# Linear attention, then a mixture-of-depths MLP: the MLP pipeline a slot earlier, the first batch's rows by a 0/1 product, loads reordered

## The chip, the cores and the metric

One NeuronCore of a Trainium2 chip (its five engines: TensorE, VectorE, ScalarE, GpSimd, and SyncE, which here only issues DMAs). The metric is the device time of one execution in microseconds. In the profile PE is TensorE's matmuls, PEld its weight loads, DVE VectorE, ACT ScalarE, POOL GpSimd, SP SyncE.

## The reference

Eight batches, eight heads, 576 positions, head dimension 64, all float32; the MLP has 512 x 1024 and 1024 x 512 weights and runs on 128 chosen rows of each batch.

```python
q_s = softmax(q, axis=-1)                    # over the 64 features
k_s = softmax(k, axis=2)                     # over the 576 positions
kv = np.einsum('bhsd,bhse->bhde', k_s, v)    # 64 x 64 for each head
x = np.einsum('bhsd,bhde->bhse', q_s, kv)    # then heads side by side: (8, 576, 512)
...
scores = np.einsum('bsd,d->bs', x, w_gate)
out = x.copy()
for b in range(B):
    top_idx = np.argpartition(-scores[b], capacity)[:capacity]     # capacity = 128
    xe = x[b, top_idx]
    ye = np.maximum(xe @ w1, 0.0) @ w2
    g = 1.0 / (1.0 + np.exp(-scores[b, top_idx]))
    out[b, top_idx] = x[b, top_idx] + g[:, None] * ye
```

## The kernel before

The work is cut into 16 *units*: a batch and four of its eight heads, so units 2b and 2b+1 make batch b. `q`, `k` and `v` of a unit lie in one of three sets of buffers (`raw`, `LD = 3`), so unit u + 3 can be loaded once unit u is read. Each unit goes through these steps:

- `load`: six DMAs on SP's queue (two each for k, v and q, 256 and 320 KB); unit 0's v goes out on ScalarE's queue.
- `k_exp`, `q_exp` (ScalarE): exponentials, k in one instruction, q in two halves; `v_copy`: v into a buffer `v_ones` that has a column of ones beside it, on VectorE or GpSimd. There are two of these buffers.
- `kv_mm` (TensorE): k and v into a PSUM bank of the tag `tp`, of which there are two; the column of ones gives the sums of k. `kv_out`: VectorE's `krec` (1/sum), ScalarE's copy to `kv_w`, then VectorE's `prod` and a reduction with the gate weights `wg`, which give the score of each row as one more column. `kv_and_exp(u)` puts `kv_mm`, half of `q_exp`, `kv_out` and the other half in this order.
- `q_t` (TensorE transposes, in two halves, and a scaled copy of each on ScalarE), `x_mm` (TensorE, two halves), `x_out` (VectorE: reciprocal, scaled rows into `xs`, score part into `sr`), `x_store`: two DMAs of the rows to the output.

Once for each batch, after its second unit: `score` (VectorE sums, and two small operations that blank rows that aren't there; GpSimd splits the score in parts of bfloat16), `score_row` (five TensorE transposes with one score column each, into two `tp` banks, and two ScalarE copies to `srow`), `compare` (five VectorE instructions that count for each row how many scores stand before it: its rank), `pick` (VectorE's `hit`, a 0/1 matrix of rank against slot number in a single buffer; five small matmuls that give the row numbers and scores of the chosen rows; GpSimd's gather of the rows from the output tensor), `gate` (the sigmoid), `turn` (four transposes of the gathered rows, copied to `xT`).

The MLP on 128 rows goes in sixteen *pieces*: eight of `mlp1` (four matmuls each, half of `hT` written by ScalarE after every four) and eight of `mlp2` (one matmul each). `finish` (VectorE's `o`, then GpSimd's scatter) ends a batch.

The order on each engine is that of the program text (`manual_schedule`). Engines run their own instructions in order, and a wait holds up everything behind it on the same engine. Slots 0 to 3 (the loop at L520, `EARLY = 4`) hold only attention, one unit each, with dummy matmuls (`fill`) between, like the 20 at the start (`WARM`); slot 2 holds the first pick. From slot 4 on (the loop at L571, `LAG = 4`) each slot holds one unit's attention between eight pieces: `mlp1` of a batch in an even slot, `mlp2` in an odd one. In such a slot the next unit's exponentials and `kv_mm` are done too; `score` stands in the odd slot, `score_row` and `compare` in the even slot after, `pick` in the odd slot after that, two pieces in. Slots 16 to 19 have only the MLP left. In slot 16 the range checks `sums_in_range` (L470) are emitted after the eight `mlp1` pieces of batch 6: twelve small VectorE operations and one matmul that sums the flags. At the end a register takes a branch by them, to a general version that doesn't run here.

The MLP's weights are loaded in slots 0 to 3: `w1` in four row blocks, `w2` in two halves. The gate weights are spread over the partitions by two DMAs of 64 KB on ScalarE's queue.

Of the kernel before, what the change touches and what calls it, by code (L numbers as in the profile page):

```python
# [17 lines left out]
def kernel(  # L18
# [20 lines left out]
    nc = tc.nc  # L39
# [18 lines left out]
    WARM = 20  # L58
# [4 lines left out]
    n_sl = -(-capacity // P)  # L63
    cuts = [capacity * i // n_sl for i in range(n_sl + 1)]
# [27 lines left out]
    def load(u, which, queue=nc.sync):  # L92
        b, qd = units[u]
        for what in which:
            src = {"q": q, "k": k, "v": v}[what]
            t = raw[what][u % LD]
            first = src[b, 4 * qd].offset
            for n, rows in ((1, N2), (0, R)):
                queue.dma_start(
                    out=t[n::2, :, :rows].rearrange("p h r d -> p h (r d)"),  # L100
                    in_=bass.AP(tensor=src.tensor, offset=first + n * R * D,
                                ap=[[9 * D, 64], [SD, 4], [1, rows * D]]))
# [5 lines left out]
    load(0, "k")  # L108
    load(0, "v", nc.scalar)
    load(0, "q")  # L110
    load(1, "kvq")
    load(2, "kvq")

# [7 lines left out]

    wg = const.tile([P, NQ, 2, D], F32, name="wg")
    for h in range(2):
        nc.scalar.dma_start(out=wg[part(h)].rearrange("p a i d -> p (a i) d"),
                            in_=bass.AP(tensor=moe_w_gate.tensor, offset=moe_w_gate.offset + h * D,
                                        ap=[[0, 64], [2 * D, 2 * NQ], [1, D]]))
    warm = const.tile([P, 1], F32, name="warm")
    nc.scalar.activation(out=warm, in_=ones_b[:, :1], func=AF.Exp)
    w1 = const.tile([P, KD, F], F32, name="w1")
    w2 = const.tile([P, KF, DM], F32, name="w2")  # L130

# [99 lines left out]
    def q_t(u, i):  # L231
# [5 lines left out]
        for r in range(R):  # L237
            for a in range(2):
# [3 lines left out]
        nc.scalar.activation(out=st["qT", u][:, i].rearrange("p r a c -> p a r c"),  # L242
                             in_=t_ps[:, :, :R * 64].rearrange("p a (r c) -> p a r c", r=R),
                             func=AF.Copy, scale=krec[:, u, i:i + 1])
# [14 lines left out]
    def x_out(u, i):  # L259
        b, qd = units[u]  # L260
        if qd == 0 and i == 0:
            xs[b] = xp.tile([P, R, NQ, 2, 2, D], F32, tag="xs", name="xs")
            sr[b] = md.tile([P, NQ * 2, G], F32, tag="sr", name="sr")
        x = st.pop(("x", u, i))[:, :, :R * C].rearrange("p h (r c) -> p h r c", r=R)
        rec = qrec[:, u, i].rearrange("p (h r) -> p h r", h=2)
        nc.vector.reciprocal(out=rec, in_=x[:, :, :, D])  # L266
        nc.vector.tensor_mul(xs[b][:, :, qd, i].rearrange("p r h d -> p h r d"), x[:, :, :, :D],  # L267
                             rec.to_broadcast([P, 2, R, D]))
        nc.vector.tensor_mul(sr[b][:, 2 * qd + i].rearrange("p (h r) -> p h r", h=2), x[:, :, :, D + 1], rec)
# [10 lines left out]
    def score(b, up=2):  # L280

        raw_s = s_all[:, b]
        nc.vector.reduce_sum(out=raw_s, in_=sr.pop(b).rearrange("p a (h r) -> p r a h", h=2),
                             axis=AX.XY)
        s = md.tile([P, R], F32, tag="s", name="s")
        nc.vector.tensor_mul(s, raw_s, valid_r[:, up])
        nc.vector.tensor_add(s, s, valid_r[:, 1])
# [8 lines left out]
    def score_row(b):  # L296
        s = st["s", b]
        srow = md.tile([P, RP], F32, tag="srow", name="srow")
        for r0, r1 in ((0, N2), (N2, R)):
            t_ps = bank("tp", 2)  # L300
            for r in range(r0, r1):
                nc.tensor.transpose(out=t_ps[:, (r - r0) * P:(r - r0 + 1) * P],
                                    in_=s[:, r:r + 1].to_broadcast([P, P]), identity=ident)
            if r0 == 0:
                nc.scalar.copy(out=srow[:, :N2 * P], in_=t_ps)
            else:
                nc.scalar.copy(out=srow[:, N2 * P:], in_=t_ps[:, :P:2])  # L307
# [43 lines left out]

    def gate(b, n):
# [9 lines left out]
    def turn(b, n):  # L362
        m = slots[n][1]
        xr = st["pick", b, n][0]
        xT = sl.tile([P, KD, P], F32, tag="xT", name="xT")
        t_ps = bank("mm", 2)
        for d in range(KD):
            nc.tensor.transpose(out=t_ps[:, d * m:(d + 1) * m], in_=xr[:m, d * P:(d + 1) * P],  # L368
                                identity=ident[:m, :m])
        nc.scalar.copy(out=xT[:, :, :m], in_=t_ps[:, :KD * m].rearrange("p (d c) -> p d c", d=KD))  # L370
# [67 lines left out]
    def general():  # L438
        for b in range(B):
# [16 lines left out]
            score_row(b)  # L456
# [33 lines left out]
    LAG = 4  # L490

    def load_w1(n):
        nc.sync.dma_start(out=w1[:, n], in_=moe_w1[n * P:(n + 1) * P])

    def load_w2(n):
        half = KF // 2
        nc.sync.dma_start(out=w2[:, n * half:(n + 1) * half],
                          in_=moe_w2[n * half * P:(n + 1) * half * P].rearrange("(f p) d -> p f d", p=P))

    EARLY = 4  # L500

# [12 lines left out]
    k_exp(0)  # L514
    v_copy(0)
    kv_and_exp(0)
    load(3, "kvq")


    for s in range(EARLY):  # L520
        q_t(s, 0)
        q_t(s, 1)
        k_exp(s + 1)
        v_copy(s + 1, nc.gpsimd)
        fill(2)
        x_mm(s, 0)
        x_mm(s, 1)
        fill(2)
        if s == 2:
            kv_mm(s + 1)  # L530
            q_exp(s + 1, 0)
            fill(3)
            pick(0)
            x_out(s, 0)
            kv_out(s + 1)
            x_out(s, 1)
            x_store(s)
            q_exp(s + 1, 1)
        else:
            x_out(s, 0)  # L540
            x_out(s, 1)
            x_store(s)
            if s == 1:
                score(0)
            kv_mm(s + 1)
            q_exp(s + 1, 0)
            kv_out(s + 1)
            if s == 1:
                score_row(0)
                for r in range(R):  # L550
                    compare(0, r)
            q_exp(s + 1, 1)
            if s == 3:
                score(1)
        fill(2)
        if s == 0:
            load_w1(0)
            load_w1(1)
        elif s == 1:
            load_w1(2)  # L560
            load_w1(3)
            load(4, "kvq")
            load(5, "kvq")
        else:
            load_w2(s - 2)
            load(s + 4, "kvq")
    each(gate, 0)
    each(turn, 0)

    number = None  # L570
    for s in range(EARLY, NU + LAG):  # L571

        mlp_b, odd = divmod(s - LAG, 2)
        piece = mlp2 if odd else mlp1
# [10 lines left out]
        last = s == NU - 1  # L585
        ends = s // 2 if here and odd else None
        compared = s // 2 - 1 if here and not odd else None
        chosen = (s - 3) // 2 if here and odd else B - 1 if s == NU else None
# [3 lines left out]
        if after:  # L592
            v_copy(s + 1)
            k_exp(s + 1)
        pieces(2)
        if chosen is not None:
            pick(chosen)
        if here:
            x_mm(s, 0)
            x_mm(s, 1)  # L600
            x_out(s, 0)
            x_out(s, 1)
            x_store(s)
        if last:
            score(ends)
        if after:
            kv_and_exp(s + 1)
        if s + 4 < NU:
            load(s + 4, "kvq")
        pieces(1)  # L610
        if last:
            compared = ends
        if compared is not None:
            score_row(compared)
            for r in range(R):
                compare(compared, r)
        if chosen is not None:
            each(gate, chosen)
        if ends is not None and not last:
            score(ends)  # L620
        pieces(4)
        if odd and mlp_b + 1 < B:
            each(turn, mlp_b + 1)
        pieces(1)
        if odd:
# [31 lines left out]
```

## Time and profile before

| | |
|---|---|
| median of three runs | 219.21 us (218.94 to 222.68) |
| the profiled execution | 217.89 us, span 216.0 us |
| TensorE waiting, matmuls from 42.6 to 209 us | 1.6 us in all |
| first `mlp1` matmul | 42.64 us |
| first gather (`xr`) | issued at 33.97 us; the transposes after it start at 41.24 us |
| last `mlp2` matmul ends | 208.79 us |
| bytes moved | 46.81 MB, mean 217 GB/s |

The costliest groups, line, engine, operation, tiles (written<-read), shapes and count, then busy time, mean duration in ns, and the idle time before them with what ended it:

```profile
L382 PE MATMUL mm<-xT,w 128*128 128x128 f32 x512 | 62.1, 278 | 0.0
L392 PE MATMUL mm<-w,hT 128*128 128x512 f32 x128 | 59.9, 603 | 0.0
L315 DVE SCALAR_TENSOR_TENSOR junk<-srow,s,not_before 128x576 bf16<-128x576 f32 x40 | 32.8, 819 | 8.3 <-ACT srow L307 7.2
L215 PE MATMUL tp<-v_ones,ke 128*64 128x65 f32 x640 | 22.6, 224 | 2.3 <-issue 2.1
L253 PE MATMUL x<-kv_w,qT 64*64 64x66 f32 x1280 | 22.4, 221 | 0.0
```

Two thirds of TensorE's time is the MLP (the two first groups). A float32 matmul is several records, and matmuls overlap, so the mean of one record is longer than its share of the stream: what a step costs is read from start to start in the timeline. In the slices of the page each digit is the busy tenths of a fortieth of the span, 5.4 us.

### The profile page before, as it was taken

The numbers are of one execution on the slowest core, as the hardware profiler recorded it, in microseconds if no ns is written. First come the engines' busy times: TensorE is split into PE (matmuls) and PEld (weight loads), VectorE is DVE, ScalarE is ACT, GpSimd is POOL, SyncE is SP. The second block draws the span as 40 slices with busy tenths as digits, with TensorE's granted clock in tenths as the row PEclk, the third lists the DMA queues.
The fourth block names the chain that finished last, engine by engine and source line by source line (L and its number), as shares of the span: only waits on it lengthen the run. The fifth ranks groups of instructions, "written<-read, shape, count | busy, mean of one in ns | idle before, by whom it ended". The sixth has DMA issues, their size and how long they took to land. (4 is left out here: it accounts for less than half of the span.)

```text
span 216.0 us, 7090 instructions
## 1 busy us (share of the span) xinstructions
PE 197.5 (91%) x3040; PEld 147.2 (68%) x3040; DVE 116.2 (54%) x359; ACT 88.6 (41%) x146; POOL 34.4 (16%) x78
## 2 busy tenths in 40 slices
PE   5987595999999999999999999999999989999960
PEld 2464462799749975897679776996599548749620
DVE  6552595668726774477626872596358665501010
ACT  2386374763626471746265443536263311211100
POOL 6022402300112012200320023001120112101010
PEclk9999999999999999999999999999999999999996
DMA  5999999999999997958594949421313041101001
GB/s 179 299 356 358 375 398 369 362 392 377 377 384 381 375 344 249 314 157 283 171 320 154 313 133 303 161 82 49 113 52 109 7 156 52 49 3 52 5 5 52
DMA packets 39335, 46.81 MB, mean 217 GB/s; under 512 B 2944, under 2 KB 36736, under 8 KB 39296
## 3 DMA queue, kind: packets, MB, share of 16 engines
q1 hardware_dynamic: 36928, 41.36, 56.4%
q0 software_dynamic: 1280, 4.20, 5.7%
q10 hardware_dynamic: 1088, 0.72, 1.1%
q8 instruction: 26, 0.43, 0.8%
q14 instruction: 13, 0.11, 0.2%
HBM read 34.73 MB, written 11.53 MB: 214 GB/s over the span
## 5 line engine op out<-in xcount | busy, mean ns | idle before, releaser
L382 PE MATMUL mm<-xT,w 128*128 128x128 f32 x512 | 62.1, 278 | 0.0
L382 PEld LDWEIGHTS mm<-xT,w 128*128 128x128 f32 x512 | 58.8, 192 | 2.3 <-ACT xT L370 1.5
L392 PE MATMUL mm<-w,hT 128*128 128x512 f32 x128 | 59.9, 603 | 0.0
L315 DVE SCALAR_TENSOR_TENSOR junk<-srow,s,not_before 128x576 bf16<-128x576 f32 x40 | 32.8, 819 | 8.3 <-ACT srow L307 7.2
L392 PEld LDWEIGHTS mm<-w,hT 128*128 128x128 f32 x128 | 22.5, 190 | 21.2 <-issue 20.4
L267 DVE TENSOR_TENSOR xs<-x,qrec 128x640 f32<-128x640 f32 x32 | 26.4, 825 | 1.1
L242 ACT ACTIVATE qT<-x,krec 128x640 f32<-128x640 f32 x32 | 23.9, 792 | 6.2 <-PE x L239 6.1
L400 DVE SCALAR_TENSOR_TENSOR o<-mm,g,xr 128x512 f32<-128x512 f32 x8 | 6.0, 751 | 37.7 <-PE mm L392 37.7
L202 ACT ACTIVATE qe<-q 128x640 f32<-128x640 f32 x32 | 23.6, 739 | 3.0 <-DMA q<-in_q_dram 2.8
L215 PE MATMUL tp<-v_ones,ke 128*64 128x65 f32 x640 | 22.6, 224 | 2.3 <-issue 2.1
L215 PEld LDWEIGHTS tp<-v_ones,ke 128*64 128x64 f32 x640 | 20.3, 137 | 5.3 <-issue 3.0
L253 PE MATMUL x<-kv_w,qT 64*64 64x66 f32 x1280 | 22.4, 221 | 0.0
L347 POOL DMA_INDIRECT xr<-out_dram,idx x8 | 8.0, 996 | 88.8 <-DVE qrec L266 72.6
L253 PEld LDWEIGHTS x<-kv_w,qT 64*64 64x64 f32 x1280 | 20.2, 134 | 2.6 <-ACT qT L242 0.8
L195 ACT ACTIVATE ke<-k 128x1280 f32<-128x1280 f32 x16 | 20.3, 1270 | 2.8 <-DMA k<-in_k_dram 2.8
L385 ACT ACTIVATE hT<-mm 128x512 f32<-128x512 f32 x16 | 9.5, 596 | 28.7 <-PE mm L382 28.7
L239 PEld LDWEIGHTS x<-ident,qe 64*128 64x128 f32 x320 | 11.7, 139 | 11.6 <-issue 5.0
L239 PE MATMUL x<-ident,qe 64*128 64x64 f32 x320 | 14.5, 229 | 4.9 <-issue 1.4
L266 DVE RECIPROCAL qrec<-x 128x10 f32<-128x10 f32 x32 | 6.9, 215 | 20.7 <-PE x L253 20.7
L401 POOL DMA_INDIRECT out_dram<-o,idx x8 | 10.1, 1269 | 46.8 <-DVE o L400 46.8
L226 ACT COPY kv_w<-tp 128x130 f32<-128x130 f32 x16 | 4.3, 266 | 31.4 <-DVE krec L224 31.4
L370 ACT COPY xT<-mm 128x512 f32<-128x512 f32 x8 | 4.7, 585 | 26.9 <-PE mm L368 26.9
(81 smaller groups left out, 126.0 us busy)
## 6 DMA issues: line engine op xcount, KB each, us to landing
k<-in_k_dram SPq DMA_DIRECT2D x16, 320.0 KB, 7.0
q<-in_q_dram SPq DMA_DIRECT2D x16, 320.0 KB, 6.1
out_dram<-xs SPq DMA_DIRECT2D x16, 320.0 KB, 2.9
v<-in_v_dram SPq DMA_DIRECT2D x15, 320.0 KB, 7.9
k<-in_k_dram SPq DMA_DIRECT2D x16, 256.0 KB, 7.2
q<-in_q_dram SPq DMA_DIRECT2D x16, 256.0 KB, 6.4
out_dram<-xs SPq DMA_DIRECT2D x16, 256.0 KB, 3.2
v<-in_v_dram SPq DMA_DIRECT2D x15, 256.0 KB, 7.7
```

The costliest lines, as they stand in the source:

```text
L195: nc.scalar.activation(out=ke, in_=raw["k"][u % LD], func=AF.Exp)
L202: nc.scalar.activation(out=st["qe", u][:, i], in_=qr[:, i], func=AF.Exp)
L215: nc.tensor.matmul(out=kv[part(h), i], lhsT=ke[:, 2 * i + h, r], rhs=vo[:, 2 * i + h, r], start=(r == 0), stop=(r == N2))
L239: nc.tensor.transpose(out=t_ps[:, a, r * 64:(r + 1) * 64], in_=qe[part(a), i, r].rearrange("p h d -> p (h d)"), identity=ident[part(a), pa ...
L242: nc.scalar.activation(out=st["qT", u][:, i].rearrange("p r a c -> p a r c"), in_=t_ps[:, :, :R * 64].rearrange("p a (r c) -> p a r c", r= ...
L253: nc.tensor.matmul(out=x[part(c), h, r * C:(r + 1) * C], lhsT=qT[part(h), i, r, c], rhs=kv_w[u % 2][part(h), i], start=True, stop=True)
L267: nc.vector.tensor_mul(xs[b][:, :, qd, i].rearrange("p r h d -> p h r d"), x[:, :, :, :D], rec.to_broadcast([P, 2, R, D]))
L315: nc.vector.scalar_tensor_tensor(junk, st["srow", b], st["s", b][:, r:r + 1], not_before[:, r], op0=OP.subtract, op1=OP.is_ge, accum_out=s ...
L382: nc.tensor.matmul(out=h_ps[:, f % 4 * m:(f % 4 + 1) * m], lhsT=w1[:, d, f * P:(f + 1) * P], rhs=xT[:, d, :m], start=(d == 0), stop=(d == ...
L385: nc.scalar.activation(out=hT[:, f - 3:f + 1, :m], in_=h_ps[:, :4 * m].rearrange("p (f c) -> p f c", f=4), func=AF.Relu)
L392: nc.tensor.matmul(out=st["y", b, n][:m], lhsT=st["hT", b, n][:, f, :m], rhs=w2[:, f], start=(f == 0), stop=(f == KF - 1))
L401: nc.gpsimd.indirect_dma_start(out=out_rows[:(b + 1) * S], out_offset=bass.IndirectOffsetOnAxis(ap=idx[:m, :1], axis=0), in_=o[:m], in_off ...
```

## The change

1. The slots: `LAG` is 3. Units 0 to 2 are written out without a loop; from slot 3 on `mlp1` stands in odd slots, `mlp2` in even ones. `score`, `score_row` and `compare` all stand in the odd slot of the batch's second unit, `pick` in the even slot after, one piece in. In slots 3 and 4 (`late`) the next unit's exponentials, `v_copy` and `kv_mm` come late in the slot; slot 3 does those of unit 3 first. `pick(0)` stands in slot 4, just ahead of `pick(1)`. In slot 16 the range checks now follow `finish(6)`.
2. The first batch's MLP input isn't gathered: `select` multiplies `xs`, still in SBUF, by a float32 0/1 matrix `hit_f` (20 matmuls), one row group after each of the five compares.
3. `x_out` is split: `x_sums` (reciprocal and score part) of both halves, then `score`, then `x_scale`. `score`'s two blanking operations go to GpSimd, `score_row` transposes the unblanked scores and ScalarE scales them in the copy.
4. Loads: unit 0's k goes out on two queues, its v on SP; `w1` in two column halves, the first right after unit 2's loads; the stores of units 0 and 1 after the scalings of unit 1.
5. The gate weights come as one row and are spread by two small matmuls with a row of ones. `q_t`'s second half of units 0 and 1 is copied by VectorE. `WARM` is 18.

```diff
-    load(0, "k")
-    load(0, "v", nc.scalar)
-    load(0, "q")
+    load(0, "k", (nc.scalar, nc.sync))
+    load(0, "vq")
     load(1, "kvq")
     load(2, "kvq")
...
+    load_w1(0)
...
+    def select(b, n, r):
+        k0, m = slots[n]
+        if r == 0:
+            st["select", n] = bank("mm", 2), md.tile([P, R, P], F32, tag="hit_f", name="hit_f", bufs=1)
+        t_ps, hit = st["select", n]
+        nc.vector.tensor_scalar(hit[:, r, :m], slot_no[:, k0:k0 + m], st["rank", b][:, r:r + 1], None, op0=OP.is_equal)
+        row = xs[b][:, r].rearrange("p a i h d -> p (a i h d)")
+        for d in range(KD):
+            nc.tensor.matmul(out=t_ps[:, d * m:(d + 1) * m], lhsT=row[:, d * P:(d + 1) * P], rhs=hit[:, r, :m],
+                             start=(r == 0 and d == 0), stop=(r == N2 and d == KD - 1), skip_group_check=True)
+        if r == N2:
+            turned(b, n, t_ps)
...
+    def ready(u, engine=nc.vector):
+        k_exp(u)
+        v_copy(u, engine)
...
+    q_t(1, 0)
+    q_t(1, 1, on_vector=True)
+    ready(2, nc.gpsimd)
+    q_exp(2, 0)
+    fill(2)
+    x_mm(1, 0)
+    x_mm(1, 1)
+    fill(3)
+    x_sums(1, 0)
+    x_sums(1, 1)
+    score(0)
+    score_row(0, tag="mm")
+    x_scale(1, 0)
+    x_scale(1, 1)
+    x_store(0)
+    x_store(1)
+    kv_mm(2)
+    for r in range(R):
+        compare(0, r)
+        for n in range(n_sl):
+            select(0, n, r)
+        if r == 1:
+            kv_out(2)
+            q_exp(2, 1)
+            q_t(2, 0)
+            q_t(2, 1)
+    load_w2(1)
+    load(5, "kvq")
+    x_mm(2, 0)
+    x_mm(2, 1)
...
+    LAG = 3
...
+        late = s < LAG + 2
+        ends = s // 2 if here and s % 2 == 1 else None
+        chosen = (s - 2) // 2 if s % 2 == 0 and s <= NU else None
+        if s == LAG:
+            x_out(s - 1, 0)
+            x_out(s - 1, 1)
+            x_store(s - 1)
+            ready(s, nc.gpsimd)
+            pieces(2)
+            kv_and_exp(s)
+            load(s + 3, "kvq")
         if here:
             q_t(s, 0)
             q_t(s, 1)
-        if after:
-            v_copy(s + 1)
-            k_exp(s + 1)
-        pieces(2)
+        if after and not late:
+            ready(s + 1)
+        pieces(1)
+        if s == LAG + 1:
+            pick(0)
         if chosen is not None:
             pick(chosen)
+        pieces(1)
         if here:
             x_mm(s, 0)
             x_mm(s, 1)
-            x_out(s, 0)
-            x_out(s, 1)
+            x_sums(s, 0)
+            x_sums(s, 1)
+            if ends is not None:
+                score(ends)
+            x_scale(s, 0)
+            x_scale(s, 1)
             x_store(s)
...
-        if after:
+        if after and not late:
             kv_and_exp(s + 1)
...
         pieces(1)
...
+        if ends is not None:
+            score_row(ends)
+            for r in range(R):
+                compare(ends, r)
         if chosen is not None:
             each(gate, chosen)
...
-        pieces(4)
-        if odd and mlp_b + 1 < B:
+        if s == LAG + 1:
+            each(gate, 0)
+        pieces(1 if s == LAG else 3)
+        if after and late:
+            ready(s + 1)
+            kv_and_exp(s + 1)
+            load(s + 4, "kvq")
+        pieces(1)
+        if second and mlp_b + 1 < B:
             each(turn, mlp_b + 1)
         pieces(1)
-        if odd:
+        if second:
             each(finish, mlp_b)
         if s == NU:
             number = sums_in_range()
```

## The prediction

> **What bounds the kernel now.** I read the page first: engine shares and the slices.
>
> ```profile
> PE 197.5 (91%) x3040; PEld 147.2 (68%) x3040; DVE 116.2 (54%) x359; ACT 88.6 (41%) x146; POOL 34.4 (16%) x78
> PE   5987595999999999999999999999999989999960
> PEclk9999999999999999999999999999999999999996
> GB/s 179 299 356 358 375 398 369 362 392 377 377 384 381 375 344 249 314 157 283 171 320 154 313 133 303 161 82 49 113 52 109 7 156 52 49 3 52 5 5 52
> ```
>
> TensorE is full from the eighth slice (about 43 us) to the end; the holes lie in the first seven, where loads run at 356 to 398 GB/s. So the kernel is load-bound, then TensorE-bound. The timeline of TensorE gives the price of a pair of full slots (q_t, two MLP pieces, x_mm, kv_mm, piece, score row, five pieces; then the mlp2 slot):
>
> ```profile
> 64.65 0.84 PE L239 MATMUL x<-ident,qe 64*128 64x64 f32 x20
> 65.42 2.05 PE L382 MATMUL mm<-xT,w 128*128 128x128 f32 x16
> 67.40 1.40 PE L253 MATMUL x<-kv_w,qT 64*64 64x66 f32 x80
> 68.73 1.39 PE L215 MATMUL tp<-v_ones,ke 128*64 128x65 f32 x40
> 70.05 1.16 PE L382 MATMUL mm<-xT,w 128*128 128x128 f32 x8
> 71.04 0.71 PE L302 MATMUL tp<-ident,s 128*128 128x128 f32 x5
> 71.59 4.63 PE L382 MATMUL mm<-xT,w 128*128 128x128 f32 x40
> 76.15 0.84 PE L239 MATMUL x<-ident,qe 64*128 64x64 f32 x20
> 78.74 0.27 PE L339 MATMUL tp<-vals,hit 128*128 128x5 bf16 x5
> 87.37 0.84 PE L239 MATMUL x<-ident,qe 64*128 64x64 f32 x20
> ```
>
> One pair is 87.37 - 64.65 = 22.72 us without a hole. From start to start: q_t 0.77, x_mm 1.33, kv_mm 1.32, a piece about 0.91 to 0.99. VectorE beside it, from its own timeline, stands just ahead of TensorE:
>
> ```profile
> 70.41 0.16 DVE L224 RECIPROCAL krec<-tp 128x2 f32<-128x2 f32 x1
> 70.91 0.29 DVE L228 TENSOR_TENSOR prod<-tp,wg 128x128 f32<-128x128 f32 x1 [0.34 <-ACT kv_w L226]
> 72.41 0.82 DVE L315 SCALAR_TENSOR_TENSOR junk<-srow,s,not_before 128x576 bf16<-128x576 f32 x1 [0.89 <-ACT srow L307]
> 76.60 0.82 DVE L205 COPY v_ones<-v 128x1280 f32<-128x1280 f32 x1
> 77.34 0.82 DVE L335 TENSOR_TENSOR hit<-slot_no,rank 128x640 bf16<-128x640 f32 x1
> ```
>
> Five compares take 76.60 - 72.41 = 4.19 us; `hit` ends 78.16, its matmul comes at 78.74: a slack of 0.6 us. The chain of waits shows the range checks in the tail, today finished as the MLP is:
>
> ```profile
> 184.60 0.39 DVE ends L478
> 186.96 0.17 PE tp L482
> 187.12 6.21 PE mm L392 x14
> ```
>
> **The change part by part.** I sum the span (216.0 us; the profiled execution is 217.89 us, so 1.89 lie around it, and it is 1.3 below the median 219.21).
>
> *To the first MLP piece.* Before, it starts at 42.64, after a gather issued at 33.97 and a transpose at 41.24. x_mm of unit 1 ends at 20.29 + 1.40 = 21.7. This part hardly moves: v of unit 1 lands just before its copy at 13.83 and its q at 15.46, both load-bound. An issue stall of 1.35 us at 18.1 may go, so 20.3 to 21.7. Below lies ScalarE: the q exponential of unit 2, which ran 21.95 to 22.69 on its load, now stands ahead of the score row's copy. From 21.7: reciprocals, sums and score 0.9, then the two scalings (2 x 0.82) on VectorE, to 24.4; transposes and copies take 1.48 (48.15 to 49.63) and end sooner. Now five rounds of compare (0.86) and a one-row `hit`. No row shows that form: it is below the 0.82 of 128x640 and above the 0.15 of a tiny operation; a fifth of the elements puts it near the lower, 0.25, with 0.1 for the wait on the rank. 5 x 1.2 = 6.0, and the kv_out of unit 2 between them 1.1 (25.93 to 27.05): 31.5. The last four select matmuls are of mlp1's form, 0.91 (the other sixteen lie under the compares: TensorE would be idle), x_mm 1.33, which covers the copy to xT (0.58). First piece at 33.8 (32.3 to 35).
>
> At this point before has done x_mm once, q_t and kv_mm twice, and a pick more: 1.33 + 1.54 + 2.64 + 0.2 = 5.7. So of 42.64 - 33.8 = 8.8 us only 3.1 are gained.
>
> Small edits: WARM by 2 (0.4), the gate weights by two small matmuls and a copy, between 0 (q lands only at 10.45) and 0.8; I take 0. Two SBUF loads of 64 KB become one row of 2 KB: 0 to -1. The second q copy of units 0 and 1 on VectorE: -0.8 to 0, hidden by unit 1's loads. POOL's two score operations (2 x 0.28) end 1.5 us before the first compare; 0.
>
> *Slot 3, from the first piece as 0.* Two pieces to 1.98, kv_mm(3) to 3.30. kv_mm, reciprocal, kv_w copy and second q exponential are now a chain in the same slot: 3.55, 3.75, 3.9 to 4.65. Second half of q_t waits from 3.7 to 4.7: **1.0**. Two pieces to 7.0, x_mm to 8.3, piece to 9.3, score row to 9.95, piece to 10.9. Then kv_mm(4). Its v copy stands on VectorE *behind* the five compares of batch 1, in program order: compares from 10.85 (scalings end, srow ends) to 15.05, copy to 15.87. TensorE waits 10.9 to 15.9: **5.0**. Loads don't hide this: by the bytes queued ahead (11 MB, at the slices' rates) unit 4 lands near 36 us, slot time 2. kv_mm 17.2, two pieces 19.2.
>
> *Slot 4.* q_t 20.0, piece 20.9, pick(0) 21.1. pick(1) needs `hit` again, a single buffer, after pick(0)'s three small operations: 21.75 + 0.82 = 22.6: **1.5**. Piece 23.7, x_mm 25.05, four pieces 28.6. kv_mm(5) waits for its v copy behind two scalings and four gate operations, 28.8: **0.25**; 30.2, piece 31.1, transpose, last piece: 32.5. The gather of batch 1 must find unit 3's rows stored; issued near 25, landing in 3.3 to 6.2 us (the eight gathers), it costs 0 to 1.5; I take 0.
>
> So slot 5 starts at 33.8 + 32.5 = 66.3. Before, the same point of the MLP was 64.65, with one unit more done: 0.77 + 1.33 + 1.32 = 3.42. Remaining: 208.79 - 64.65 + 3.42 = 147.6, to 213.9.
>
> *Full slots.* Score and score row now lie in the slot of x_mm. Against x_mm's start (67.40 before): sums end 2.0, score 2.3, scalings to 3.8, krec 3.70 (was 3.01), kv_w, prod ends 4.50. The fifth transpose of the score row needs the bank that prod reads: 4.08 becomes 4.55, **0.45**. Behind it wait five pieces. First compare 5.5 (was 5.01); `hit`, after the v copy, ends 11.2; TensorE is at pick at 11.34 - 0.91 (a piece fewer before it) + 0.47 = 10.9: **0.4**. Five pairs x 0.85 = 4.25 (0 if VectorE runs half a microsecond ahead of this, as it did before; 6 if as much behind).
>
> *End.* Without kv_mm(16) and with the pick a piece into slot 16, waits there are some 0.5, where 167.0 to 208.8 now holds about 1.2: -0.7. But slot 16 is now the second slot of its batch: on VectorE `o` of batch 6 stands before the range checks, and their matmul stands on TensorE before mlp1 of the last batch. Price: `o` 0.75 + checks 184.52 to 186.91 = 2.39 + about 0.1 = **3.2**, where it was 0.17.
>
> *The clock.* Windows after the last matmul (PE ends 208.79; columns: window, length, five engines' busy time and count, granted clock, DMA share, GB/s):
>
> ```profile
> 208.80:211.50 2.70, 0.00 (x0) 0.00 (x0) 0.75 (x1) 0.00 (x0) 0.97 (x1) 1.00 0.08 26
> 211.50:216.00 4.50, 0.00 (x0) 0.00 (x0) 0.00 (x0) 0.00 (x0) 0.00 (x0) 0.58 0.13 48
> ```
>
> A hole of 2.1 us (23.5 to 25.56) left the clock at 1.00; this one of 7.2 lowers it after more than 2.7. The first dummy matmuls came each 0.43 us until 7.38 and then each 0.20: half speed for 5.1 us. So the new hole of 5.0 us costs between 0 and 5.1 / 2 = 2.5; I take 1.2, as 5.0 lies between the two holes. The 3.2 us hole: 0.
>
> The Trainium skill, "TensorE: Matmul & The Clock Gate", Part 1, says that the clock halves after an idle window of about 3.4 us, free-running, and returns after as long a busy one; that speaks against this change, as its hole passes the window. By the page the price, an estimate, would be 0 (window not met) or 3.4 / 2 = 1.7 us, the sum 227.8 or 229.5 in place of 229.0.
>
> Sum: 213.9 + 4.25 - 0.7 + 3.2 + 7.2 (tail from 208.79) + 1.2 = 229.0, time 230.9, 13 over the profiled 217.89. The median lies somewhat above a profiled run (1.3 here), but the chains above take every wait in full and the start at its late bound; I set **231**.
>
> **Rivals.**
>
> *Loads land early enough to pay for all waits* (not slower). Place: q of unit 2 on ScalarE ahead of the score row. For: the first two slices move only 179 and 299 GB/s, and small gate packets go. Price: each us earlier is one off the end. To come to +2% (223.6) T0 must fall by 7.4 us, so q must land by 14.5 instead of 21.95: 5.3 MB by 14.5 is 366 GB/s from time zero, the steady rate without any start-up. Decides there: below 14.5 same, below 9 faster. Time then 214 to 223. Against: both slices' shape is start-up.
>
> *Full slots hide their waits*: VectorE's 0.4 us per pick and 0.45 per score row vanish: 231 - 4.3 = 226.7. For: margins are tenths. Against: the order on VectorE is fixed and TensorE's slack was 0.6.
>
> *Both holes lower the clock, and the gather comes late*: + 1.3 + 1.6 + 1.5 = 235.4.
>
> *The MLP doesn't start sooner*: issue stalls like those at 18.1 and 23.5 (1.35 and 2.1) hit the select loop instead, T0 36: 233.
>
> **How the numbers follow.** My sum, 228 to 233: 0.50. Full slots hide their waits: 0.13. Clock and gather: 0.10. Late start: 0.10. Loads early: 0.17, of which 0.06 is faster. What a measurement tells from no change is about 2%, 214.8 to 223.6. So faster 0.06, same 0.11, slower 0.83. Range 223 to 235.5, leaving out most of the early loads below 223 (0.14) and a little above.
>
> **What would show it.** First mlp1 matmul near 33.8; in slot 3 a TensorE hole of about 5 us ahead of kv_mm, ended by the v copy after five compares, with a granted clock under 1.00 after it; one of 1.5 between two picks; holes of about 0.4 at each fifth transpose and each pick; one of 3.2 at the checks' matmul before the last mlp1. Wrong would be a first piece before 30, or a page in which TensorE is full between 34 and 66 us.

## The result and the profile after

The changed kernel takes 234.0 us (median of 4 runs, 233.8 to 234.4) where the kernel before, on the same chip, takes 220.3 (4 runs, 218.9 to 222.7): a ratio of 1.064, interval 1.056 to 1.073. (Ratios leave out runs in which the chip was in its slower state, here the one of 222.7 us.) Its profiled execution is 234.13 us with a span of 231.7. The page of the changed kernel, to be held against the same rows of before:

```profile
PE   6985698839799999999999999999999999859980
PEclk9999999976999999999999999999999999997998
```

The slices show both places at once. The dip to 3 in the PE row is the ninth slice (46 to 52 us), and the clock row falls to 7 and 6 there; a second dip, a 5, stands at 203 to 208 us, with a 7 in the clock row one slice later. The list of what TensorE waited for names them:

```profile
PE tp L227 <- DVE v_ones L217: 5.0, 1, 5.0
PE tp L524 <- DVE good L521: 3.1, 1, 3.1
PE tp L363 <- DVE hit L359: 3.0, 7, 1.2
```

The columns behind the colon are the sum in us, the number of waits and the longest. TensorE's timeline of the changed kernel gives each wait its place (start, length, and in brackets the idle time ahead):

```profile
34.29 2.05 PE L424 MATMUL mm<-xT,w 128*128 128x128 f32 x16
...
44.17 1.06 PE L424 MATMUL mm<-xT,w 128*128 128x128 f32 x8
50.24 2.44 PE L227 MATMUL tp<-v_ones,ke 128*64 128x65 f32 x40 [5.01 <-DVE v_ones L217]
52.60 3.51 PE L424 MATMUL mm<-xT,w 128*128 128x128 f32 x16
...
59.28 0.28 PE L363 MATMUL tp<-vals,hit 128*128 128x5 bf16 x5 [1.24 <-DVE hit L359]
...
69.12 0.83 PE L251 MATMUL x<-ident,qe 64*128 64x64 f32 x20
...
75.50 1.05 PE L326 MATMUL tp<-ident,s_all 128*128 128x128 f32 x5
...
83.00 0.28 PE L363 MATMUL tp<-vals,hit 128*128 128x5 bf16 x5 [0.16 <-DVE hit L359]
...
92.61 0.83 PE L251 MATMUL x<-ident,qe 64*128 64x64 f32 x20
...
208.81 0.17 PE L524 MATMUL tp<-good,ones_b 128*1 128x6 bf16 x1 [3.15 <-DVE good L521]
208.91 9.04 PE L424 MATMUL mm<-xT,w 128*128 128x128 f32 x64
```

The first mlp1 piece starts 8.4 us sooner than before (34.29 against 42.64). The first pair of full slots takes 92.61 - 69.12 = 23.49 us, before 22.72. Behind the hole of 5.01 kv_mm takes 2.44 instead of 1.39 and two pieces take 3.51 instead of 2.05. The windows of the changed kernel say why (length, the busy time and count of PE, PEld, DVE, ACT and POOL, granted clock, DMA share, GB/s):

```profile
47.20:50.20 3.00, 0.00 (x0) 0.00 (x0) 2.82 (x7) 0.00 (x0) 0.00 (x0) 0.78 1.08 387
50.20:52.60 2.40, 2.36 (x40) 2.28 (x40) 0.00 (x0) 0.00 (x0) 0.00 (x0) 0.50 1.08 372
52.60:56.04 3.44, 3.44 (x18) 3.32 (x17) 1.48 (x4) 0.90 (x2) 0.00 (x0) 0.55 1.08 375
...
207.50:209.00 1.50, 0.19 (x2) 0.10 (x1) 1.15 (x7) 0.00 (x0) 0.23 (x1) 1.00 0.45 175
209.00:213.40 4.40, 4.40 (x25) 4.40 (x26) 0.29 (x2) 0.00 (x0) 0.00 (x0) 0.61 0.03 6
```

The clock is halved until nearly 56 us, and again for most of 209 to 213.4. VectorE's timeline of the changed kernel shows what TensorE waits for in the first hole: the last of five compares, and only behind it the copy of v.

```profile
48.52 0.82 DVE L339 SCALAR_TENSOR_TENSOR junk<-srow,s,not_before 128x576 bf16<-128x576 f32 x1
...
49.27 0.82 DVE L217 COPY v_ones<-v 128x1280 f32<-128x1280 f32 x1
```

### The profile page after: what moved, and what is told of

It reads as the page before. It is cut to its first block, busy times and chain, and to the rows that moved or that the text cites. A ratio compares the mean times of both kernels' runs of the same rounds, so it can differ in the third digit from the quotient of the medians.

```text
span 231.7 us, 7142 instructions
## 1 busy us (share of the span) xinstructions
PE 204.8 (88%) x3058; PEld 153.1 (66%) x3062; DVE 120.7 (52%) x353; ACT 86.8 (37%) x144; POOL 36.0 (16%) x93
## 4 chain that ended last, share of the span: by engine, by line
PE 50%; DVE 22%; DMA 15%; ACT 4%; issue 4%; SPq 1%; POOL 1%; POOLq 0%; DVEq 0%; ACTq 0%
PE mm L434 23%; PE mm L424 11%; DVE junk L339 11%; DMA q<-in_q_dram 9%; PE x L268 7%; PE tp L227 4%; DMA k<-in_k_dram 3%; DVE xs L290 3%; DMA v<-in_v_dram 3%; PE x L251 2%; DVE hit L359 2%; DVE v_ones L217 2%; ACT qe L214 2%; SPq L100 1%; PE mm L405 1%
## 5 line engine op out<-in xcount | busy, mean ns | idle before, releaser
L424 PE MATMUL mm<-xT,w 128*128 128x128 f32 x512 | 65.9, 287 | 0.0
L424 PEld LDWEIGHTS mm<-xT,w 128*128 128x128 f32 x512 | 62.3, 201 | 4.4 <-issue 3.2
L434 PE MATMUL mm<-w,hT 128*128 128x512 f32 x128 | 61.6, 608 | 0.0
L434 PEld LDWEIGHTS mm<-w,hT 128*128 128x128 f32 x128 | 22.0, 190 | 17.6 <-issue 16.7
L227 PE MATMUL tp<-v_ones,ke 128*64 128x65 f32 x640 | 23.5, 230 | 6.9 <-DVE v_ones L217 5.0
L227 PEld LDWEIGHTS tp<-v_ones,ke 128*64 128x64 f32 x640 | 21.1, 143 | 9.7 <-issue 8.7
L290 DVE TENSOR_TENSOR xs<-x,qrec 128x640 f32<-128x640 f32 x32 | 24.9, 815 | 0.0
L259 ACT ACTIVATE qT<-x,krec 128x640 f32<-128x640 f32 x30 | 22.3, 790 | 5.7 <-PE x L251 5.7
L443 POOL DMA_INDIRECT out_dram<-o,idx x8 | 9.6, 1201 | 74.4 <-DVE o L442 74.4
L371 POOL DMA_INDIRECT xr<-out_dram,idx x8 | 8.7, 1086 | 63.4 <-DVE no L369 43.1
```

The costliest lines, as they stand in the source:

```text
L227: nc.tensor.matmul(out=kv[part(h), i], lhsT=ke[:, 2 * i + h, r], rhs=vo[:, 2 * i + h, r], start=(r == 0), stop=(r == N2))
L259: nc.scalar.activation(out=to, in_=src, func=AF.Copy, scale=krec[:, u, i:i + 1])
L424: nc.tensor.matmul(out=h_ps[:, f % 4 * m:(f % 4 + 1) * m], lhsT=w1[:, d, f * P:(f + 1) * P], rhs=xT[:, d, :m], start=(d == 0), stop=(d == ...
L434: nc.tensor.matmul(out=st["y", b, n][:m], lhsT=st["hT", b, n][:, f, :m], rhs=w2[:, f], start=(f == 0), stop=(f == KF - 1))
L443: nc.gpsimd.indirect_dma_start(out=out_rows[:(b + 1) * S], out_offset=bass.IndirectOffsetOnAxis(ap=idx[:m, :1], axis=0), in_=o[:m], in_off ...
```

## The experiments

The theory: the head start at the first piece is worth about 3 us, and is given away by the order of instructions on VectorE (two holes, with the low clock behind them, and two small waits in each pair of slots). The main rivals: the holes cost nothing beyond what would be late next, or the loads or the 0/1 product are what costs. Four groups of runs were each made beside runs of the kernel before on one chip. Levels differ between chips (the kernel before took 224.5 us beside the first four runs, 219.0 to 219.8 beside the others), so times are compared by their ratio to the kernel before. The changed kernel itself wasn't run on the chip of the first four runs: that its ratio is 1.064 there too is assumed, and a difference of two ratios is good to 2 or 3 us at best. For e1 to e4 the argument therefore rests on the waits and durations in their profiles, and the ratios only agree with it.

**e1: v of unit 4 copied by GpSimd**

```diff
 # slot 3, ahead of kv_mm(4)
-            ready(s + 1)
+            ready(s + 1, nc.gpsimd if s == LAG else nc.vector)
```

> Slot 3's copy of unit 4's v goes to GpSimd, so it no longer stands on VectorE behind the five compares. Theory (the copy in program order makes the 5.0 us hole, and the hole lowers the clock): kv_mm of unit 4 waits only for its k exponential, which ends at 46.1 in the trace of the changed kernel; a hole of 1 to 1.5 us is left at 45.1, the clock stays at 1.00, and the time falls by 5.0 - 1.3 for the hole and 2.5 for the clock: by about 6 us, from 234.0 to 228. Rival (the loads set this stretch: DMA share is full from 34 to 55 us): the hole moves to the next step that needs unit 4 or 5, and the time falls by 2 us or less.

Measured: ratio 1.025 (1.015 to 1.035), 230.6 us. The timeline of this kernel, all engines:

```profile
44.64 1.85 POOL L217 COPY v_ones<-v 128x1280 f32<-128x1280 f32 x1
46.54 1.39 PE L227 MATMUL tp<-v_ones,ke 128*64 128x65 f32 x40 [1.83 <-POOL v_ones L217]
47.86 2.05 PE L424 MATMUL mm<-xT,w 128*128 128x128 f32 x16
```

The hole shrinks to 1.83 (the copy now stands behind GpSimd's seven score operations, and takes 1.85 instead of 1.25), and kv_mm and the two pieces behind it have their full speed. From the first piece to the start of slot 5 it is 30.76 us (33.77 to 64.53) instead of 34.83: 4.1 less, where hole and clock together give 5.7; 1.2 is given back to two waits that the changed kernel hadn't, 0.40 at q_t(4) and 0.81 at the turn of batch 1, for its gather. By the ratios the gain is 8.7 us (3 either way), more than the 6 expected; 1.6 of it is the last mlp1, which by chance kept its clock here (see the end). The order of the v copy behind the compares is shown as the cause of the hole.

**e2: the range checks ahead of `finish`**

```diff
 # end of slot 16
+        if s == NU:
+            number = sums_in_range()
         if second:
             each(finish, mlp_b)
-        if s == NU:
-            number = sums_in_range()
```

> In slot 16 the range checks are emitted ahead of the last vector step of batch 6, as they stood relative to it before the change. Theory: the hole of 3.15 us before the checks' matmul goes, and the slow stretch behind it (the 64 records of the next mlp1 took 8.87 us instead of 7.28) with it: by 4.7 us, to 229.3. Rival (that stretch is slow for another reason than the idle time): by 3.1 us, to 230.9. Second rival (VectorE's checks then hold the last vector step of batch 6 and its scatter): no gain.

Measured: ratio 1.041 (1.032 to 1.051). From the timeline of this kernel:

```profile
209.62 0.17 PE L524 MATMUL tp<-good,ones_b 128*1 128x6 bf16 x1
209.72 7.41 PE L424 MATMUL mm<-xT,w 128*128 128x128 f32 x64
```

The wait at L524 is gone from the list; the other waits stand as they were (5.0 ahead of kv_mm(4), picks 2.7). Against the changed kernel's 1.064 that is some 5 us; its hole (3.15) and the slow mlp1 behind it (9.04 us there, 7.41 here) are together 4.8, and the clock behind the first hole cost 0.8 less in this profile. The hole is the order on VectorE, not the checks' own work.

**e3: the holes filled with dummy matmuls**

```diff
 # slot 3, ahead of ready(4) and kv_mm(4)
+        if s == LAG:
+            fill(23)
 # end of slot 16, ahead of sums_in_range
+        if s == NU:
+            fill(14)
```

> The two holes stay, but dummy matmuls fill them: 23 of 0.216 us in slot 3 and 14 in slot 16, ahead of the instruction that waits. Theory (the granted clock falls because TensorE is idle): kv_mm of unit 4 still starts at about 50.2 and the checks' matmul at about 208.8 less what was gained before, but kv_mm takes 1.4 instead of 2.44 and the two pieces after it 2.05 instead of 3.51, and the mlp1 after the checks 7.3 instead of 8.87; the time falls by 2.5 + 1.6 = 4.1 us, to 229.9. Rival (full DMAs or something else slows these stretches): the durations stay and the time stays at 234.

Measured: ratio 1.045 (1.037 to 1.054). Windows of this kernel at the first hole, then its timeline at the first and the second:

```profile
44.00:49.00 5.00, 4.95 (x27) 2.51 (x27) 4.69 (x12) 2.15 (x4) 0.47 (x3) 1.00 1.08 377
49.00:51.40 2.40, 2.35 (x47) 1.82 (x46) 0.66 (x2) 0.14 (x1) 0.00 (x0) 1.00 1.07 373
```

```profile
49.63 1.39 PE L227 MATMUL tp<-v_ones,ke 128*64 128x65 f32 x40
50.95 2.05 PE L424 MATMUL mm<-xT,w 128*128 128x128 f32 x16
...
210.50 7.41 PE L424 MATMUL mm<-xT,w 128*128 128x128 f32 x64
```

kv_mm(4) starts as long after the first piece as in the changed kernel (15.95 us in both), but TensorE is busy in the wait, and the clock stays at 1.00: kv_mm and the pieces behind it are 1.05 and 1.46 shorter, the last mlp1 1.63. Together 4.1; the ratio fell by 0.019, 4.2 us. This prices the clock apart from the holes.

**e4: VectorE's order in the full slots**

```diff
 # even slots: the v copy behind the pick; odd slots: the scalings behind kv_out
-            ready(s + 1)
+            k_exp(s + 1)
...
             pick(chosen)
+        if after and not late:
+            v_copy(s + 1)
...
-            x_scale(s, 0)
-            x_scale(s, 1)
-            x_store(s)
         if after and not late:
             kv_and_exp(s + 1)
+        if here:
+            x_scale(s, 0)
+            x_scale(s, 1)
+            x_store(s)
```

> In the full slots VectorE scales the rows after kv_out instead of before it, and copies the next v after the pick instead of before it. Theory (five pairs of slots pay for these two orders): the waits at the fifth transpose and at the pick go, a pair takes 22.7 to 22.9 us instead of 23.5 to 23.9, and the time falls by 3.5 to 4.4 us, to about 230. Rival (the extra time of a pair lies in the stream of matmuls that is cut into shorter runs by the new positions, not in VectorE): at most 1 us.

Measured: ratio 1.050 (1.039 to 1.061). Odd slots fall from 11.83 to 11.50 us, and the score row's transposes have their 0.71 again; the waits of the picks in full slots are gone (the 1.25 between the two picks of slot 4 and 0.61 in slot 16 stay). The gain in the odd slots is as large as the wait that was taken away. The even slots took 12.0 to 12.5 us, since x_mm was broken by issue stalls beside the gather on that chip (0.4 us each, in all four kernels), so the ratio alone doesn't settle the pairs; e5 does, on a chip without these stalls.

**c1: the changed kernel again, on another chip**

> The changed kernel once more, beside the runs of this call, because the kernel before took 224.5 us beside the first four experiments and 220.3 beside the changed kernel. Theory (the ratio carries over): 1.055 to 1.07 of the kernel before. Rival (the machine of the first four runs slowed both by the same microseconds in their full slots): the same ratio within the interval, but x_mm in the mlp2 slots again broken by an issue stall.

Measured: ratio 1.064 (1.055 to 1.073), pairs of 23.5, 23.9, 23.5, 23.5 and 23.5 us without an issue stall in x_mm: the stalls of the first four runs aren't part of the change. The ratio carries over between two chips on which the kernel before takes about the same (220.3 and 219.7); for the chip where it takes 224.5 that isn't shown.

**e5: all orders mended at once**

```diff
 # e2 and e4, and besides:
             q_t(s, 0)
             q_t(s, 1)
+        if after and late:
+            ready(s + 1, nc.gpsimd)
...
-        if s == LAG + 1:
+        if s == LAG:
             pick(0)
...
         if after and late:
-            ready(s + 1)
             kv_and_exp(s + 1)
```

> The changed kernel with its waits mended together: checks ahead of the last vector step of batch 6; rows scaled after kv_out and v copied after the pick; units 4 and 5 made ready right after q_t with v on GpSimd; the first pick in slot 3 instead of beside the second. Theory (these waits are the whole loss): 5.0 + 2.5 (slot 3 and its clock) + 1.2 (two picks) + 4.7 (checks and clock) + 4.0 (full slots) = 17.4 us off the changed kernel, so 0.985 to 0.995 of the kernel before. Rival (what is left is load-bound or lies in a later start elsewhere): 1.01 to 1.03.

Measured: 220.5 us, ratio 1.007 (1.004 to 1.010). Nearly all of the 6.4% comes back, by reordering and by giving two copies of v to GpSimd, but the kernel isn't ahead of the one before: the time lies between the theory (0.985 to 0.995) and its rival (1.01 to 1.03). Five pairs take 114.8 us (63.62 to 178.42), where the changed kernel takes 118.0: 3.2 of the 4.4 lost there was VectorE's order. Its timeline shows a new wait in slot 4:

```profile
49.65 0.17 DVE L236 RECIPROCAL krec<-tp 128x2 f32<-128x2 f32 x1
49.85 0.27 ACT L238 COPY kv_w<-tp 128x130 f32<-128x130 f32 x1 [4.86 <-DVE krec L236]
50.02 0.74 ACT L214 ACTIVATE qe<-q 128x640 f32<-128x640 f32 x1
...
50.81 0.53 PE L251 MATMUL x<-ident,qe 64*128 64x64 f32 x10 [2.44 <-ACT qe L214]
```

kv_mm(4) no longer waits, but its reciprocal still stands behind the five compares; ScalarE's kv_w copy waits for that for 4.86 us, the q exponential stands behind the copy, and the second half of q_t waits 2.44 us. Behind this shorter hole, too, the clock is at 0.57 (52.4 to 56.4 us), at a price of 1.7.

**e6: the kernel before with the first loads changed** (k of unit 0 on two queues, its v on SP, the gate weights as a row spread by matmuls; `w1` and the stores stay as before)

```diff
-    load(0, "k")
-    load(0, "v", nc.scalar)
-    load(0, "q")
+    load(0, "k", (nc.scalar, nc.sync))
+    load(0, "vq")
...
```

> The kernel before with one part of the change alone: unit 0's k on two queues, its v on SP's, and the gate weights as one row spread by two small matmuls. Theory (TensorE's full stretch starts at 42.6 us behind a gather, and the issue stall of 1.35 us at 18 us sets x_mm of unit 1): unit 2 lands 2 to 3 us earlier, the time falls by 0 to 1 us. Rival (the first stage is bound by these loads): first full slot 2 us earlier and the time 2 us less.

Measured: ratio 1.003 (0.999 to 1.007), 219.8 us. The first mlp1 piece starts at 43.81, before at 42.64. These loads alone bring nothing. The order of `w1` and of the stores, the split of `x_out`, VectorE's copies in q_t and WARM weren't run by themselves.

**e7: the changed kernel without the 0/1 product** (the first batch picked, gathered and turned ahead of slot 3)

```diff
-        for n in range(n_sl):
-            select(0, n, r)
...
+    pick(0)
     x_mm(2, 0)
     x_mm(2, 1)
+    each(turn, 0)
...
-        if s == LAG + 1:
-            pick(0)
```

> The changed kernel without the 0/1 product: the first batch's rows are picked after its five compares, gathered and transposed, as before the change; the rest stays. Theory (the product is what brings the first piece forward): compares end near 28.5, the gather starts near 31 but finds the stores of units 0 and 1 landed only near 36 to 38, and takes 4 to 6 us more: first piece at 42 to 44 instead of 34.3; TensorE's stream is late by 8, of which the hole of 5.0 in slot 3 may give nothing back as it hangs on the same start: 7 to 9 us slower than the changed kernel, about 242. Rival (the loads bound the following slots anyway): less than 3 us slower.

Measured: 248.8 us, ratio 1.136 (1.129 to 1.143), the first piece at 49.32. From the list of TensorE's waits:

```profile
PE mm L405 <- DMA xr<-out_dram,idx: 13.1, 1, 13.1
```

In this order the product is worth some 15 us, about twice what was expected: the pick's matmul runs at 31.7, but the gather is issued only at 41.1 and lands at 47.5, while 383 GB/s are moved (34 to 47.5 us). The clock is at 0.50 from 32 us on, behind a wait of 2.74 for the pick, and at 0.53 until 53. The rival (less than 3 us slower) falls.

**e8, e9: the wait in slot 4 mended**

```diff
 # e8, on e5
-            for r in range(R):
+            for r in range(2 if s == LAG else R):
                 compare(ends, r)
...
             kv_and_exp(s + 1)
             load(s + 4, "kvq")
+        if s == LAG:
+            for r in range(2, R):
+                compare(ends, r)
 # also: a piece between the halves of q_t(3); the picks of batch 1 and of the last batch later
 # e9, on e8: v of unit 3 on VectorE
+    v_copy(3)
     load_w2(1)
     load(5, "kvq")
     x_mm(2, 0)
...
-            ready(s, nc.gpsimd)
+            k_exp(s)
```

> The all-mended kernel with three more places moved: in slot 3 unit 4's sums and their kv_out stand after the second of the five compares instead of behind all five, and the second half of q_t(3) stands behind a piece of mlp1; the pick of batch 1 stands behind x_mm(4), and the pick of the last batch one piece later. Theory: the waits that the all-mended kernel still had go (2.44 at the second half of q_t(4), 0.75 at q_t(3), 0.6 at the last pick), and with the 2.44 the low clock behind it (x_mm(4) 2.07 to 1.40 us, one stretch of mlp2 2.03 to 1.02: 1.7). That is 5.5 us of its span of 218.3: span 212.8 to 214, ratio to the kernel before 0.980 to 0.990, slot 5 at 59.0 to 60.0 (63.6). Rival: the three compares that now stand behind kv_out end later, so that the pick of batch 1 and its gather come late for the turn at the end of slot 4, which then waits 1 to 2 us: ratio 0.993 to 0.998. Rival: the clock falls for another reason than the hole; then x_mm(4) stays near 2.1 and slot 5 starts after 60.7.

> The kernel with slot 4 mended, and the copy of v of unit 3 moved from GpSimd to VectorE, behind the last of the 0/1 columns. In two of seven profiles a hit_f column took 1.36 and 1.15 us instead of 0.29 where that GpSimd copy ran beside it. Theory: the two contend, and the column is on the chain to the first piece of mlp1, so all five columns take 0.29 here and the first mlp1 stays between 33.0 and 33.6; the copy on VectorE is covered by the 2 us for which VectorE waits for x_mm(2). Time against the kernel with slot 4 mended: 0 to -1 us, ratio 0.995 to 1.0. Rival: the copy on VectorE pushes x_sums(2) and krec(3) back, and the time is 0.8 us longer. Rival: the long columns come from something else, and one of them is long here too.

Measured: e8 223.7 us, ratio 1.019 (1.014 to 1.024); e9 222.8, 1.018 (1.013 to 1.023). The waits it was to remove are gone (q_t(4) 0, the last pick 0), 78 of the 80 records of x_mm(4) take 1.39 again (the last two come after a new stall of 0.98 on issue, of which the trace shows no cause), and the kernel, expected at 0.980 to 0.990, is slower than e5 by 1.2%. The timeline of e8:

```profile
49.75 1.70 SPq L300 DMA_DIRECT2D out_dram<-xs  x2
...
57.16 1.02 POOL L371 DMA_INDIRECT xr<-out_dram,idx  x1 [8.54 <-DMA out_dram<-xs]
...
63.23 1.11 PE L405 MATMUL mm<-ident,xr 128*128 128x128 f32 x4 [4.25 <-DMA xr<-out_dram,idx]
64.14 1.92 PE L434 MATMUL mm<-w,hT 128*128 128x512 f32 x2
65.98 1.33 PE L251 MATMUL x<-ident,qe 64*128 64x64 f32 x20
67.24 2.93 PE L424 MATMUL mm<-xT,w 128*128 128x128 f32 x16
```

TensorE now reaches the turn of batch 1 before its gather has landed. The gather waits for the store of unit 3's rows, which is issued at 49.75 behind six loads. The wait is 4.25 us, and the four steps after it run at a low clock. In e5 the same gather had been issued at 57.4, but TensorE, held up by the 2.44, came to the turn when it had landed: the earlier wait covered this one. (It also landed in at most 4.8 us there, 57.40 to 62.23, and in 6.0 here.) The rival of a late gather was right in kind, but it came through the store, not the pick. In e9 all five `hit_f` columns take 0.29 us and the first piece starts at 33.38; the gain over e8 is 0.4%, within the intervals.

**e10: that store ahead of the loads**

```diff
 # slot 3, on e9
             kv_and_exp(s)
-            load(s + 3, "kvq")
...
             x_store(s)
+            if s == LAG:
+                load(s + 3, "kvq")
```

> The kernel with v of unit 3 on VectorE, and in slot 3 the store of unit 3's rows stands ahead of the loads of unit 6 on SP's queue instead of behind them. Theory: the 4.3 us for which the turn of batch 1 waited in slot 4 is the gather of batch 1, which could not start before 57.2 because that store was issued at 49.8, behind six loads, and landed at 57; with the store issued at about 44.5 the gather starts when its list is there (53.5), lands by 59, and the wait goes; with it the low clock behind it (the stretch of 64 to 70: L405 1.11 to 0.60, mlp2 1.92 to 1.02, q_t(5) 1.33 to 0.83, mlp1 2.93 to 2.05: 2.8). Span 221.3 less 3.8 less 2.8: 214 to 216, ratio to the kernel before 0.985 to 0.995. Rival: the transfers as a whole are the bound up to 60 (359 to 394 GB/s in every slice from 5 to 65), so the loads of unit 6, or the gather itself, are late by what the store gains: a new wait of 2 us or more at unit 6's k or v or again at the turn, span 218 or more, ratio 1.00 or above.

Measured: 217.6 us (12 runs) against 219.8 (16 runs), ratio 0.992 (0.988 to 0.996): the one version here that is ahead of the kernel before, by 0.8%, as expected (0.985 to 0.995). The timeline of e10:

```profile
54.32 1.03 POOL L371 DMA_INDIRECT xr<-out_dram,idx  x1 [6.46 <-DMA q<-in_q_dram]
...
60.25 0.66 PE L405 MATMUL mm<-ident,xr 128*128 128x128 f32 x4 [0.68 <-DMA xr<-out_dram,idx]
60.74 1.02 PE L434 MATMUL mm<-w,hT 128*128 128x512 f32 x2
```

The gather starts 2.8 us sooner than in e8, TensorE waits 0.68 for it, and the granted clock is 1.00 from 53 to 66 us. One store (two DMAs) moved past six loads on a queue is worth 2.6% by the ratios of e9 and e10, and 5.4 us by their spans (221.3 and 215.9).

## Why the prediction was right, and where it was off

The forecast (231, range 223 to 235.5, slower) holds the measured 234.0. By its steps:

| step of the prediction | predicted | measured |
|---|---|---|
| first mlp1 piece | 33.8 | 34.29 |
| second half of q_t(3) waits | 1.0 | 0.75 |
| hole ahead of kv_mm(4) | 5.0 | 5.01 |
| between two picks in slot 4 | 1.5 | 1.24 |
| kv_mm(5) waits | 0.25 | 0 |
| five pairs of full slots, over 22.72 each | 4.25 | 4.4 (118.0 in all) |
| hole at the checks | 3.2 | 3.15 |
| clock behind the first hole | 1.2 | 2.5 (1.7 to 2.8 in five profiles) |
| clock behind the second hole | 0 | 1.6 (0 to 2.9 in five profiles) |
| tail after the last matmul | 7.2 | 6.9 |
| span | 229.0 | 231.7 |

*To the first piece.* Right, though not by its reasons throughout. Unit 2 landed sooner than assumed: v could be copied at 17.54 (20.33 before), and the q exponential ran at 20.31 (21.95). It didn't help: the issue stall that the prediction let go (1.35) stayed, at 1.76 us, and x_mm(1) started at 20.63 (20.29 before). So the rival of early loads falls: q's exponential ran 1.6 us earlier, far from the 14.5 us that the rival needed, and the time to the first piece didn't follow; in e6 the first loads by themselves don't bring it forward either. (Its bound for a faster kernel was wrong too: at one us for each us, 214.8 needs q by some 6 us, not by 9.) `hit_f`, for which no row existed, takes 0.29, beside the 0.25 that was estimated. A round of compare and `hit_f` takes 1.06 us instead of 1.2, and one column of 1.36 us takes the gain back: that the sum came out within 0.5 is in part luck.

*Slots 3 and 4.* The hole ahead of kv_mm(4) and its cause were right to a tenth. e1 shrinks it by moving the copy, and only 1.2 us of other waits take its place.

*Full slots.* The two terms, 0.45 at the fifth transpose and 0.4 at the pick, were right as a sum: odd slots take 11.83 us instead of 11.50, 0.33 more, and even slots 11.66 to 12.07 instead of 11.22, 0.55 more in the mean. e4 shows the odd slot's part, and e5, with 22.8 to 23.2 us a pair, that most of both is VectorE's order. The rival that these waits are hidden falls with the pairs' 23.5 to 23.9 us in the changed kernel, in two profiles.

*The mis-sized term is the clock.* The mechanism was right, its size wasn't. The prediction placed the 5.0 us hole between holes of 2.1 and 7.2 and took 1.2 of at most 2.5, and 0 for the 3.2 us hole. Measured are 2.5 and 1.6, 2.9 more than it took; the span came out 2.7 longer, so the other terms nearly cancel. e3 shows that it is the clock and that the idle time lowers it, since with the same waiting and a busy TensorE both prices vanish. The rival "both holes lower the clock, and the gather comes late" (235.4) was right in its first half; the gather wasn't late in this kernel, but became so in e8, where slot 4 is shorter.

The page "TensorE: Matmul & The Clock Gate" of the Trainium skill, Part 1, gives a free-running window of about 3.4 us, and an estimate from it was 0 or 1.7 for the first hole. The measured 2.5 lies above it, and the holes of 3.15 us here and 2.44 in e5 lie under that window and still cost 1.6 and 1.7; there the measurement decides.

*Where the head start goes.* e10 has the piece 8.95 us sooner than before and its last mlp2 starts at 201.94, where before it was 201.74: 9.15 us are used up in between. (The profiled spans are 215.9 and 216.0; the two profiled executions lie 0.7 above the median of e10 and 1.9 below that of the kernel before, so they don't show the 0.8%.) The prediction's 5.7 us of attention work that merely moves behind the first piece is the largest part; the pairs (22.8 to 23.2 instead of 22.72) take 1.1, and the stalls and waits left in slots 3 and 4 (0.47, 0.97 and 0.68) 2.1. That makes 8.9. The close match is chance: by starts in the timeline slots 3 and 4 take some 1.6 us more than work and waits explain, a third of it in the eight pieces of mlp1, which stand in shorter runs (8.1 us, before 7.5), and the 1.5 us that the kernel before waits in slots 15 and 16 are gone. By the 5.7, an estimate, the most that this change could bring was about 3 us, and only where nothing is lost in VectorE's and SP's order.

## What to carry to other kernels

When a stage is pulled forward, list for each in-order queue what now stands ahead of each short instruction that another engine waits for: here one copy of 0.82 us behind five compares cost 7.5 us, and one store behind six loads some 5. A hole on TensorE can cost more than its length (0 to 2.9 us more here), so give dummy work to those that can't be removed. And before starting, count what the earlier start merely moves behind it: of 8.4 us only about 3, by the estimate, could be gained.

## What was not expected of the hardware

*The price of the clock after a hole varies, and why is open.* The same hole of 3.15 us ahead of the last mlp1 was followed in five profiles by 64 matmul records of 7.41 (e1), 8.90 (c1), 9.04 (the changed kernel), 10.09 (e4) and 10.31 us (e7): a price of 0 to 2.9. The 5.01 us hole ahead of kv_mm(4) cost 1.7 (e2), 1.9 (c1), 2.5, 2.6 (e4) and 2.8 us (e7). Two of the first five, from the timelines of e1 and of e7:

```profile
207.79 0.17 PE L524 MATMUL tp<-good,ones_b 128*1 128x6 bf16 x1 [3.15 <-DVE good L521]
207.88 7.41 PE L424 MATMUL mm<-xT,w 128*128 128x128 f32 x64
```

```profile
223.90 0.17 PE L524 MATMUL tp<-good,ones_b 128*1 128x6 bf16 x1 [3.15 <-DVE good L521]
223.99 10.31 PE L424 MATMUL mm<-xT,w 128*128 128x128 f32 x64
```

Holes of 1.83 us (e1) and 2.09 (before) cost nothing, the 2.44 us one of e5 did. The same page calls its window free-running, so that the moment of a change of clock depends on where in the window the work falls. A price that varies could come from that; but a hole of 3.15 us can't fill a window of 3.4, and no run here moved a hole to try it.

*GpSimd and VectorE hold each other up.* From the timeline of the changed kernel, VectorE and GpSimd:

```profile
25.20 0.29 DVE L382 TENSOR_SCALAR hit_f<-slot_no,rank 128x128 f32<-128x128 f32 x1
...
26.26 1.36 DVE L382 TENSOR_SCALAR hit_f<-slot_no,rank 128x128 f32<-128x128 f32 x1
26.29 1.25 POOL L217 COPY v_ones<-v 128x1280 f32<-128x1280 f32 x1 [1.75 <-DMA v<-in_v_dram]
```

The `hit_f` column that meets the copy of v takes 1.36 us and ends 0.08 after it. The same happened in e2 (1.15); in c1 the column began 0.13 us before the copy and kept its 0.29. Likewise a compare beside such a copy took 1.68 in e8 and 1.81 in e5 instead of 0.82, while the copies themselves stretched to as much as 1.85. The Trainium skill, "SBUF — State Buffer", section "Who interferes with whom", has VectorE and GpSimd take turns at a shared pair of ports for a whole instruction, the copies, tensor_scalar and operations with two inputs in SBUF among them, which agrees with these rows. The remedy for a short operation on the critical path is to keep GpSimd's long copies away from it, as e9 does.
